# The token sums of a feed-forward block, written and streamed in interleaved orders

## The chip, the cores and the metric

The kernel runs on one core of a Trainium2 chip. The metric is the device time of one execution in microseconds (us). Two runs of the kernel before took 615.34 and 617.78 us, a median of 616.56 us.

## The reference

For 2048 tokens of 512 channels it mixes two branches with a gate per token:

```
x = A_x                                            # 2048 x 512
g = sigmoid((x * gate_w).sum(-1))
a = attention(x @ wqkv) @ wo                       # 32 heads of 16; each token sees itself and 7 tokens before, 2 apart
b = (gelu(x @ w_gate) * (x @ w_up)) @ w_down       # 512 -> 1792 -> 512
out = g * a + (1 - g) * b
```

All is float32. The change is in the operands of `x @ w_gate` and `x @ w_up`.

## The kernel before

**Tiling.** The tokens are split by parity (even and odd); each parity has 1024 tokens, in two blocks of 512. The 512 channels are four chunks of 128, and a chunk's 128 channels lie on the 128 partitions, so that a tile of x is 128 channels by 512 tokens. The 1792 hidden channels are 14 blocks of 128 (f in the code).

**Precision.** A float32 matmul is made from operands rounded to fewer bits (fp32r). Each operand is split (lines 82 to 87): ScalarE writes the rounded value `hi` (line 86), and VectorE the rest, `raw - hi` (line 87), as `lo`. A product is then three matmuls: hi by hi, hi of the weights by lo of the tokens, lo of the weights by hi of the tokens.

**Gate and up.** x times the two weight blocks of an f is taken as a 2 by 2 by 2 block product: token block by channel half, times channel half by gate or up. It is done with seven block products in place of eight (Strassen's method in Winograd's form). For this, four sums of the token blocks are needed: with a11, a12 the first token block's channel halves and a21, a22 the second's, s1 = a21 + a22, s2 = s1 - a11, s4 = a12 - s2, s3 = a11 - a21. A channel half is two chunks (kc = 0, 1), so there are eight tiles of sums. `sums_x` (lines 125 to 138) computes them on VectorE, in place, and splits each into the tile pair `XOP[name, kc]`: one tile of 1024 columns with the tag S, hi in the first 512 and lo in the last. It does so once for each token parity: before the value projection of the even tokens, and beside the key and query projection of the odd ones.

`gate_up` (lines 537 to 588) makes the seven products of one f. Four of them stream a sum (s1, s2, s4, s3), three stream a token block's half as it is (a11, a12, a22). Each call of `product` (lines 475 to 481) is six matmuls into one PSUM bank: for each of two chunks, the three of the split. The weights are the stationary operand, 128 by 128; the tokens are the moving operand, 128 by 512, one column for each token:

```python
            for n, (w_, a_) in enumerate(((wh, ah), (wh, al), (wl, ah))):
                LAST[:] = [nc.tensor.matmul(ps, w_, a_, start=(start and kc == 0 and n == 0),
```

So a sum's tiles are written once for each parity, and read by 42 matmuls (14 blocks of f times 3).

**Around it.** `ffn` runs the 14 blocks of a parity. Between the products of block f it places the down projection of earlier blocks (`down`, line 520), ScalarE's and VectorE's work on the results (lines 485 to 497, 555, 570, 586), and the preparation of the next weights (`fetch`, `combine`, `operands`, `down_w`). The attention's work on VectorE (lines 288 to 339) is a generator from which `pull` takes a bit at a time, by a written cost for each step. `paced` adds an order after the last matmul recorded, which is no wait on a value. The order of the instructions on each engine comes from this program order, as the tile framework's scheduler sets it.

Of the kernel before, what the change touches and what calls it, by code (L numbers as in the profile page):

```python
# [44 lines left out]
def tile_gated_mix(ctx: ExitStack, tc: tile.TileContext, xt, wqkv, wff, wo, out):  # L45
    nc = tc.nc
# [10 lines left out]
    def tl(tag, dt=F32):  # L57
        return pool.tile([P, COLS.get(tag, 512)], dt, name=tag, bufs=BUFS[tag])

    def pair(tag):  # L60
        t = tl(tag, F32R)
        return t[:, :512], t[:, 512:1024]
# [19 lines left out]
    def split(eng, hi, lo, raw, copy=None):  # L82
        if copy:
            copy(hi, raw)
        else:
            nc.scalar.activation(hi, raw, AF.Copy)
        eng.tensor_tensor(lo, raw, hi.bitcast(F32), op=OP.subtract)
# [13 lines left out]
    X, XOP, XR, WC = {}, {}, {}, {}  # L101
    LAST = []

    def fetch_x(par, kc):

        raw = XR[kc] = tl("raw")
        for blk in range(2):
            nc.sync.dma_start(raw[:, blk * 1024:blk * 1024 + 1024].rearrange("p (a c) -> p a c", a=2),
                                xt[2 * par + blk, :, kc:kc + 3:2, :])
# [14 lines left out]

    def sums_x():

        for n in ("s1", "s2", "s4", "s3"):
            for kc in range(2):
                XOP[n, kc] = pair("S")
        for kc in range(2):  # L130
            a11, a12, a21, a22 = (XR[kc][:, i * 512:(i + 1) * 512] for i in range(4))
            nc.vector.tensor_tensor(a22, a21, a22, op=OP.add)
            nc.vector.tensor_tensor(a21, a11, a21, op=OP.subtract)
            nc.vector.tensor_tensor(a11, a22, a11, op=OP.subtract)
            nc.vector.tensor_tensor(a12, a12, a11, op=OP.subtract)
            for n, x in ("s1", a22), ("s2", a11), ("s4", a12), ("s3", a21):
                split(nc.vector, *XOP[n, kc], x)
                yield

    def rooms():  # L140
# [333 lines left out]

    def product(ps, a, w, start):
        for kc in range(2):
            ah, al = XOP[a, kc]
            wh, wl = (x[:, kc * P:(kc + 1) * P] for x in w)
            for n, (w_, a_) in enumerate(((wh, ah), (wh, al), (wl, ah))):
                LAST[:] = [nc.tensor.matmul(ps, w_, a_, start=(start and kc == 0 and n == 0),  # L480
                                            stop=(kc == 1 and n == 2), skip_group_check=True)]

    def copy(ps):
        s = tl("s")
        nc.scalar.activation(s, ps, AF.Copy)  # L485
        return s
# [50 lines left out]
    def gate_up(par, f, pieces, do):  # L537
# [13 lines left out]
        idle(0, 0.0)  # L551
        X_ = bank("p")
        product(X_, "a11", w["b11"], True)
        W_ = bank("p")
        nc.scalar.activation(W_, X_, AF.Copy)
        idle(1, 0.7)
        piece(0)
        Z_ = bank("p")
        product(Z_, "s1", w["t1"], True)
        p5 = copy(Z_)  # L560
        idle(2, 0.3)
        fourth()
        product(X_, "s2", w["t2"], False)
        u2 = copy(X_)
        idle(3, 0.7)
# [57 lines left out]
    def ffn(par):  # L623
# [3 lines left out]
        for f in range(FC):  # L627
# [24 lines left out]
            if par:  # L652
                if f + 2 < FC:
                    at(0, fetch_sums, f + 2)
                else:
                    at(0, fetch_o) if f + 2 == FC else None
                if f + 1 == FC:
                    todo = chain(load_o(), channels_of(0, 0))
                    for i in range(1, 9):
                        at(i, next, todo, None)  # L660
            else:
                if f + 2 < FC:
                    at(1, fetch, f + 2)
                    at(8, combine, f + 2)
                else:
                    at(0, fetch_x, 1, f + 2 - FC)
                if f + 1 < FC:
                    do.setdefault(0, []).insert(0, lambda: keep(f + 1))
                at(0, keep_parts, f)
                if f + 2 == FC:  # L670
                    at(8, early)
                if f + 1 == FC:
                    todo = before()
                    for i in range(2, 9):
                        at(i, next, todo, None)
# [119 lines left out]
    for kc in range(KC):  # L795
# [4 lines left out]
        for blk in range(2):  # L800
            for a, n in first if not blk else ((0, 512),):
                o = (2 * blk + kc // 2) * 512 + a
# [16 lines left out]
    for _ in sums_x():  # L819
        pass  # L820
# [19 lines left out]
    for kc in range(KC):  # L840
        load_cb(1, kc, "c", room)()
    project(1, 0, sums_x())
    for kc in range(KC):
        load_cb(2, kc, "r", room, True)()
# [48 lines left out]
```

## Time and profile before

| | |
|---|---|
| runs | 615.34 and 617.78 us, median 616.56 |
| span of the profiled execution | 614.2 us |
| TensorE (PE) busy | 604.1 us, 98% |
| TensorE weight loads (PEld) busy | 505.3 us, 82% |
| VectorE (DVE) busy | 513.7 us, 84% |
| ScalarE (ACT) busy | 376.9 us, 61% |
| GpSimd (POOL) busy | 82.5 us, 13% |
| matmuls of line 480 that stream a sum | 672, mean 389 ns each |
| matmuls of line 480 that stream a token block | 504, mean 390 ns each |

The profile is of one execution. Its span goes from the first to the last instruction, 614.2 us; its own time isn't listed apart from the two runs, and the fastest of them is 1.1 us above the span. Matmuls are pipelined: one of 389 ns begins before the one before it has ended, so the pace is read from the distance of their starts and not from their durations. PEld, the load of the stationary operand, overlaps PE. In a row of a group stand line, engine, operation, what is written and read, shapes, count; then busy time, the mean of one, and the idle time of the engine just before them with what ended it.

### The profile page before, as it was taken

What the parts mean: (1) busy time and instruction counts of PE and PEld (TensorE: products, weight loads), DVE (VectorE), ACT (ScalarE), POOL (GpSimd) and SP (SyncE); (2) the same over time, 40 slices, a digit from 0 to 9 for tenths busy, and PEclk for the clock granted to TensorE, in tenths of its full rate; (3) what the DMA queues carried; (4) which work ended last, traced back from release to release, by engine and by line L of the source; (5) the groups of instructions that cost most, each with busy time, mean ns of one, the idle gap of its engine ahead of it and who ended that gap; (6) DMA issues with size and microseconds to landing.
All of it is one profiled execution on the core that took longest, in us unless ns stands there. A gap on an engine that the chain in (4) does not pass through costs nothing.

```text
span 614.2 us, 8246 instructions
## 1 busy us (share of the span) xinstructions
PE 604.1 (98%) x2839; PEld 505.3 (82%) x2839; DVE 513.7 (84%) x598; ACT 376.9 (61%) x633; POOL 82.5 (13%) x110
## 2 busy tenths in 40 slices
PE   9999998999999999999999999999999999999997
PEld 7899886877878888888889888888888888888885
DVE  6849699878998888756698998899899889797972
ACT  6554545674867877857356439447756676685632
POOL 0061011120212121101100002101011101101300
PEclk9999999999999999999999999999999999999999
DMA  8398949797889988995639969787888769937724
GB/s 286 98 252 253 319 145 299 192 262 226 204 225 277 305 210 219 280 231 179 237 93 330 305 174 266 210 235 186 238 200 221 162 225 215 268 86 206 91 64 154
DMA packets 85591, 132.48 MB, mean 216 GB/s; under 512 B 8111, under 2 KB 52271, under 8 KB 85550
## 3 DMA queue, kind: packets, MB, share of 16 engines
q1 hardware_dynamic: 63742, 94.27, 46.9%
q0 software_dynamic: 12672, 32.84, 28.1%
q10 hardware_dynamic: 9136, 4.85, 2.6%
q8 instruction: 22, 0.36, 0.3%
q14 instruction: 19, 0.16, 0.1%
HBM read 67.18 MB, written 36.77 MB: 169 GB/s over the span
## 4 chain that ended last, share of the span: by engine, by line
PE 81%; issue 8%; DMA 7%; DVE 3%; ACT 0%; POOL 0%; SPq 0%; POOLq 0%; DVEq 0%; ACTq 0%
PE p L480 35%; PE acc L191 15%; PE acc L520 11%; PE p L520 11%; PE p L742 5%; PE p L191 4%; DMA raw<-wff 3%; PE acc L742 2%; DMA g<-raw 2%; DMA d<-r 1%; DVE prod L326 1%; DMA raw<-xt 1%; DMA ws<-raw 1%; DVE raw L423 0%; DVE prod L330 0%
## 5 line engine op out<-in xcount | busy, mean ns | idle before, releaser
L480 PE MATMUL p<-S,g 128*128 128x512 f32 x672 | 166.6, 389 | 0.8 <-DVE c L490 0.8
L480 PEld LDWEIGHTS p<-S,g 128*128 128x128 f32 x672 | 126.0, 188 | 27.3 <-DVE c L490 1.3
L480 PE MATMUL p<-A,g 128*128 128x512 f32 x504 | 127.4, 390 | 2.9 <-ACT g L446 1.2
L480 PEld LDWEIGHTS p<-A,g 128*128 128x128 f32 x504 | 94.2, 188 | 23.9 <-DMA g<-raw 1.8
L288 DVE TENSOR_TENSOR prod<-kq 128x2048 f32<-128x2048 f32 x32 | 73.1, 2284 | 13.2 <-DMA kq<-kq 5.9
L326 DVE TENSOR_TENSOR prod<-v,lg 128x2048 f32<-128x2048 f32 x32 | 73.0, 2281 | 6.4 <-DMA v<-vs 4.9
L442 POOL DMA_DIRECT2D g<-raw x42 | 36.4, 867 | 298.3 <-ACT g L441 145.5
L291 DVE TENSOR_REDUCE lg<-prod 128x128 f32<-128x2048 f32 x32 | 73.0, 2282 | 0.3
L520 PE MATMUL p<-d,hh 128*128 128x512 f32 x224 | 68.6, 389 | 0.0
L520 PE MATMUL acc<-d,hh 128*128 128x512 f32 x224 | 60.7, 390 | 1.1 <-DMA d<-r 1.1
L520 PEld LDWEIGHTS acc<-d,hh 128*128 128x128 f32 x224 | 42.0, 188 | 10.4 <-DMA d<-r 1.4
L446 ACT ACTIVATE g<-raw 128x1024 fp32r<-128x1024 f32 (+1 forms) x42 | 41.3, 988 | 13.1 <-PE p L480 12.8
L520 PEld LDWEIGHTS p<-d,hh 128*128 128x128 f32 x224 | 42.0, 188 | 8.8
L490 DVE TENSOR_TENSOR c<-p,s 128x512 f32<-128x512 f32 x56 | 38.2, 685 | 12.9 <-PE p L480 12.6
L441 ACT ACTIVATE g<-raw 128x1024 fp32r<-128x1024 f32 (+1 forms) x42 | 41.3, 983 | 9.9 <-DVE raw L423 9.5
L485 ACT ACTIVATE s<-p 128x512 f32<-128x512 f32 x56 | 33.1, 593 | 21.4 <-PE p L480 21.2
L497 DVE TENSOR_TENSOR hl<-c,hh 128x512 fp32r<-128x512 f32 x56 | 38.0, 679 | 9.3 <-ACT hh L496 9.3
L494 DVE TENSOR_TENSOR c<-c 128x512 f32<-128x512 f32 x56 | 38.3, 685 | 8.4 <-ACT c L586 7.9
L520 PE MATMUL p<-d,hl 128*128 128x512 f32 x112 | 42.9, 389 | 0.0
L496 ACT ACTIVATE hh<-c 128x512 fp32r<-128x512 f32 x56 | 35.1, 626 | 9.7 <-DVE c L494 9.2
L533 ACT ACTIVATE rt<-p 128x512 f32<-128x512 f32 x48 | 27.9, 594 | 20.2 <-PE p L520 20.1
L191 PE MATMUL acc<-g,A 128*128 128x258 f32 (+2 forms) x228 | 39.5, 306 | 0.0
(146 smaller groups left out, 912.1 us busy)
## 6 DMA issues: line engine op xcount, KB each, us to landing
g<-raw POOLq DMA_DIRECT2D x28, 512.0 KB, 7.3
raw<-wff SPq DMA_DIRECT2D x42, 256.0 KB, 3.8
ws<-g SPq DMA_DIRECT2D x14, 768.0 KB, 5.5
g<-ws SPq DMA_DIRECT2D x14, 768.0 KB, 6.6
r<-wff SPq DMA_DIRECT2D x28, 256.0 KB, 4.3
d<-r POOLq DMA_DIRECT2D x28, 256.0 KB, 6.4
g<-raw POOLq DMA_DIRECT2D x14, 384.0 KB, 5.9
v<-vs SPq DMA_DIRECT2D x8, 512.0 KB, 7.7
```

The costliest lines, as they stand in the source:

```text
L191: LAST[:] = [nc.tensor.matmul(ps[:, :cn], a[:, t], w[:, c0:c0 + cn], start=(kc == 0 and n == 0), stop=(kc == KC - 1 and n == 2))]
L288: paced(nc.vector.tensor_tensor(prod, spans(k, jj), q[:, jj:jj + 2, None, :].to_broadcast([P, 2, W, UC]), op=OP.mult))
L291: nc.vector.tensor_reduce(two_of(lg, jj), prod.rearrange("p j w (h d) -> p (j w) h d", d=DH), axis=AX.X, op=OP.add)
L326: paced(nc.vector.tensor_tensor(prod.rearrange("p j w (h d) -> p (j w) h d", d=DH), spans(v, jj).rearrange("p j w (h d) -> p j w h d", d=D ...
L441: nc.scalar.activation(lo, raw, AF.Copy, scale=-1.0)
L446: ins = nc.scalar.activation(hi, raw, AF.Copy)
L480: LAST[:] = [nc.tensor.matmul(ps, w_, a_, start=(start and kc == 0 and n == 0), stop=(kc == 1 and n == 2), skip_group_check=True)]
L490: nc.vector.tensor_tensor(c, ps, s, op=OP.add)
L494: nc.vector.tensor_tensor(ge, ge, up, op=OP.mult)
L497: nc.vector.tensor_tensor(hl_, ge, hh_.bitcast(F32), op=OP.subtract)
L520: LAST[:] = [nc.tensor.matmul(pp, a[:, ts], w, start=(i == 0 and n == 0 and gr == 0), stop=(i == 1 and n == 2), skip_group_check=True)]
L742: LAST[:] = [nc.tensor.matmul(pa, a, b, start=(first and n == 0), stop=(last and n == 2), skip_group_check=True)]
```

## The change

A table gives an order (h, b) for 15 of the 16 sums (four names, two chunks, two parities); the s3 of the odd tokens' first chunk has none. When `sums_x` splits a sum, hi and lo are written to other columns than before, and `product` reads them with an access pattern that yields the tokens in their old order. Results and PSUM layouts stay as they were.

With b above 1 a tile of 512 columns is h regions of 512 / h columns; tokens are dealt out to the regions in runs of b. Order (2, 4), for instance, puts tokens 0 to 3 into the first half, 4 to 7 into the second, 8 to 11 into the first, and so on; whoever reads the tokens in order takes four neighbouring words, hops 256 columns (1024 bytes) on, takes four, and hops back. With b = 1 the tokens are written h columns apart, and read with a step of h words: every second or every fourth word, in two or four passes over the tile.

```diff
+    ORDER = {(0, "s1", 0): (2, 2), (0, "s1", 1): (2, 4), (0, "s2", 0): (2, 8), (0, "s2", 1): (2, 16),
+             (0, "s4", 0): (2, 32), (0, "s4", 1): (4, 2), (0, "s3", 0): (4, 4), (0, "s3", 1): (4, 16),
+             (1, "s1", 0): (2, 64), (1, "s1", 1): (8, 2), (1, "s2", 0): (8, 4), (1, "s2", 1): (4, 8),
+             (1, "s4", 0): (2, 1), (1, "s4", 1): (4, 1), (1, "s3", 1): (16, 2)}
+    SEEN = {}
+
+    def seen(t, n, kc):
+
+        o = SEEN.get((n, kc))
+        if o is None:
+            return t
+        h, b = o
+        if b == 1:
+            return t.rearrange("p (a h) -> p h a", h=h)
+        return t.rearrange("p (h a b) -> p a h b", h=h, b=b)
+
+    def shaped(t, n, kc):
+        o = SEEN.get((n, kc))
+        if o is None:
+            return t
+        h, b = o
+        if b == 1:
+            return t.rearrange("p (h a) -> p h a", h=h)
+        return t.rearrange("p (a h b) -> p a h b", h=h, b=b)
+
...
     def sums_x():
 
+        par = 1 if SEEN else 0
+        SEEN.clear()
+        SEEN.update({(n, kc): o for (q, n, kc), o in ORDER.items() if q == par})
         for n in ("s1", "s2", "s4", "s3"):
...
             for n, x in ("s1", a22), ("s2", a11), ("s4", a12), ("s3", a21):
-                split(nc.vector, *XOP[n, kc], x)
+                split(nc.vector, *(seen(y, n, kc) for y in XOP[n, kc]), shaped(x, n, kc))
                 yield
...
     def product(ps, a, w, start):
         for kc in range(2):
-            ah, al = XOP[a, kc]
+            ah, al = (seen(y, a, kc) for y in XOP[a, kc])
             wh, wl = (x[:, kc * P:(kc + 1) * P] for x in w)
```

A name of ORDER is (token parity, sum, chunk). The a11, a12 and a22 operands have no order, and are read as before.

## The prediction

> **What bounds the kernel now.** I read the page's first part, the slices and the chain of the work that ended last, in that order.
>
> ```profile
> PE 604.1 (98%) x2839; PEld 505.3 (82%) x2839; DVE 513.7 (84%) x598; ACT 376.9 (61%) x633; POOL 82.5 (13%) x110
> ...
> PE   9999998999999999999999999999999999999997
> ...
> PEclk9999999999999999999999999999999999999999
> ...
> PE 81%; issue 8%; DMA 7%; DVE 3%; ACT 0%; POOL 0%; SPq 0%; POOLq 0%; DVEq 0%; ACTq 0%
> PE p L480 35%; PE acc L191 15%; PE acc L520 11%; PE p L520 11%; PE p L742 5%; PE p L191 4%; DMA raw<-wff 3%; PE acc L742 2%; DMA g<-raw 2%; DMA d<-r 1%; DVE prod L326 1%; DMA raw<-xt 1%; DMA ws<-raw 1%; DVE raw L423 0%; DVE prod L330 0%
> ```
>
> TensorE is busy for 604.1 of 614.2 us, in every slice, at the full granted clock throughout, and the chain is TensorE for 81%. The largest part of the chain is line 480, the gate and up products. The change is about that line's streamed operand. So the first question is how much room the stage has, and I asked for the busy time by stage (columns: the stage, its length, then PE, PEld, DVE, ACT and POOL busy with their instructions, clock, DMA share, GB/s) and for what TensorE waits for.
>
> ```profile
> 18.00:60.00 42.00, 42.00 (x277) 38.73 (x276) 31.22 (x42) 21.35 (x53) 11.90 (x20) 1.00 0.72 202
> 60.00:120.00 60.00, 57.70 (x253) 47.07 (x252) 51.21 (x57) 33.00 (x51) 6.03 (x7) 1.00 0.86 249
> 120.00:180.00 60.00, 57.42 (x249) 46.21 (x249) 54.71 (x66) 40.06 (x65) 10.33 (x12) 1.00 0.87 226
> 180.00:240.00 60.00, 60.00 (x267) 49.69 (x266) 51.08 (x65) 47.22 (x74) 11.02 (x13) 1.00 0.88 240
> ...
> 300.00:330.00 30.00, 30.00 (x191) 27.18 (x190) 28.58 (x37) 19.91 (x43) 2.96 (x5) 1.00 0.65 199
> 330.00:400.00 70.00, 70.00 (x343) 59.38 (x342) 64.29 (x67) 35.95 (x62) 6.90 (x8) 1.00 0.87 248
> 400.00:460.00 60.00, 60.00 (x267) 49.67 (x266) 57.15 (x59) 38.10 (x61) 6.06 (x7) 1.00 0.82 215
> ```
>
> In the feed-forward stages TensorE has 2.30 us of gaps between 60 and 120 us, 2.58 between 120 and 180, and none after. Whatever a matmul of line 480 takes longer is therefore added to the time nearly one to one; whatever it takes shorter is gained only until VectorE (57.15 of 60 us in the later stages) becomes the bound.
>
> **The change, part by part.** Instruction for instruction, the built program has the same work in the same order on all five engines; no transfer is added or moved and no wait. What differs is the form of 15 of the 16 pairs of split instructions that write the sums (line 86 on ScalarE, line 87 on VectorE) and the order in which line 480 streams those sums. With h and b as the change's table gives them, a sum lies in h regions, and its reader takes b neighbouring words from each region in turn; for b = 1 it reads every h-th word. I sort the fifteen by the length of their runs: lone words 8 bytes apart, (2, 1), and 16 bytes apart, (4, 1); runs of two, four sums; of four, three; of eight, two; of 16 and more, four. One sum of the odd tokens (s3, first channel chunk) stays as it was.
>
> *The matmuls.* Their number and present price:
>
> ```profile
> L480 PE MATMUL p<-S,g 128*128 128x512 f32 x672 | 166.6, 389 | 0.8 <-DVE c L490 0.8
> L480 PEld LDWEIGHTS p<-S,g 128*128 128x128 f32 x672 | 126.0, 188 | 27.3 <-DVE c L490 1.3
> L191 PE MATMUL acc<-g,A 128*128 128x258 f32 x96 | 14.7, 284 | 0.0
> ```
> ```profile
> 191.35 2.72 PE p L480 x12
> ```
>
> 672 matmuls stream a sum: 16 sums (four names, two chunks, two parities) times 14 blocks times 3, so 42 for each sum, and 630 get a new order. Twelve take 2.72 us, 0.227 us from one to the next. From 258 to 512 columns an instruction grows from 284 to 389 ns, so a column streams in 105 / 254 = 0.413 ns, and the other 15 ns of the 227 are fixed.
>
> No moving operand in the trace before has a hop in it, so the price of a hop is bounded from both sides. Below: nothing, if the operand port takes any order, or even a gain of the 15 fixed ns, for which I see no reason. Above: the pace at which the other readers of the same memory take words.
>
> ```profile
> L446 ACT ACTIVATE g<-raw 128x1024 fp32r<-128x1024 f32 x28 | 29.7, 1060 | 11.8 <-PE p L480 11.5
> ...
> L446 ACT ACTIVATE g<-raw 128x768 fp32r<-128x768 f32 x14 | 11.8, 843 | 1.3 <-PE p L480 1.3
> ```
> ```profile
> L330 DVE TENSOR_TENSOR prod<-prod 128x1024 f32<-128x1024 f32 x32 | 39.0, 1219 | 0.4
> ...
> L332 DVE TENSOR_TENSOR prod<-prod 128x512 f32<-128x512 f32 x32 | 22.0, 688 | 0.5
> ```
>
> ScalarE takes a word in (1060 − 843) / 256 = 0.85 ns, VectorE in (1219 − 688) / 512 = 1.04 ns. TensorE's weight load is the slowest reader here: 128 columns in 188 ns, 1.47 ns a column, all of its fixed part counted. So line 480 is the one consumer that moves words of four bytes more than twice as fast as any other, and if that pace comes from neighbouring words being fetched together, it is the first to lose it when runs get short. I take that: runs of two and lone words 8 bytes apart fall to ScalarE's 0.85 ns, the nearest row above 0.413; lone words 16 bytes apart, which share nothing, fall to the weight load's 1.47; runs of four words and longer cost nothing.
>
> A matmul at 0.85 ns takes 512 × 0.435 = 0.223 us more, one at 1.47 ns 512 × 1.056 = 0.541 us more. Five sums (four with runs of two, and (2, 1)) are 210 matmuls: +46.8 us. The (4, 1) sum is 42 matmuls: +22.7 us. Together +69.5 us. Of the even tokens' share (two sums, 84 matmuls, 18.7 us) I take 3 us as covered by the 4.9 us of gaps shown above: what TensorE waits for there arrives at its old time while TensorE is later. The odd tokens' stages have no gap to fill. The sum is **+66.5 us**.
>
> VectorE and ScalarE are no limit then: their work in the longer stages is the same, so their shares fall, and what was late behind them (c of line 490, 0.8 us before the sums' matmuls) is late no more. The next wait is again the matmul before.
>
> *The splits.* Fifteen on each of the two engines now write with hops.
>
> ```profile
> L87 DVE TENSOR_TENSOR S<-raw,S 128x512 fp32r<-128x512 f32 x22 | 14.3, 680 | 0.0
> ...
> L87 DVE TENSOR_TENSOR hl<-raw,hh 128x512 fp32r<-128x512 f32 x8 | 5.3, 684 | 6.5 <-ACT hh L86 6.5
> ```
> ```profile
> L86 ACT ACTIVATE S<-raw 128x512 fp32r<-128x512 f32 x22 | 13.3, 629 | 10.9 <-DVE raw L134 7.3 <-DMA raw<-os 1.8 <-DVE raw L135 1.6
> ...
> L86 ACT ACTIVATE hh<-raw 128x512 fp32r<-128x512 f32 x8 | 4.8, 628 | 10.7 <-DMA raw<-os 9.1 <-PE acc L742 1.5
> ```
>
> The hh and hl rows are splits too, from line 723, and they already write in another order than they read, in runs of 32 words: 684 against 680 ns and 628 against 629 ns, so hops between long runs are free there. Short runs aren't shown; between nothing and a doubling they cost 15 × (0.629 + 0.680) = 19.6 us on two engines at most. On the path this is nothing:
>
> ```profile
> L480 PE MATMUL p<-S,g x672: 388/389/500, 59.3 to 555.6; 128*128 128x512 f32 x168
> ```
> ```profile
> 30.22 0.69 DVE L87 TENSOR_TENSOR S<-raw,S 128x512 fp32r<-128x512 f32 x1
> ```
> ```profile
> 321.66 0.67 DVE L87 TENSOR_TENSOR S<-raw,S 128x512 fp32r<-128x512 f32 x1
> ```
> ```profile
> 343.64 1.52 PE L480 MATMUL p<-S,g 128*128 128x512 f32 x6
> ```
>
> The last even sum is done at 30.9 us and first streamed at 59.3; the last odd one at 322.3 and 343.6. Doubling even all eight even and seven odd pairs, one engine after the other, takes 10.5 and 9.2 us, inside 28 and 21 us, while TensorE is busy without a gap with line 191 (42.00 of 42.00 and 30.00 of 30.00 us above). Were that cover gone, at most the 5 us that one engine loses in one parity would show.
>
> **The sum.** The profiled execution spans 614.2 us; the two runs have a median of 616.56, 2.4 us more for what lies around the span. 616.56 + 66.5 gives **683 us**. The forecast's own range is 670 (the 16-byte sum at ScalarE's pace too: 252 × 0.223 − 3 = +53) to 703 (210 matmuls at VectorE's 1.04 ns, +0.320 us each, and the same 22.7: +87).
>
> **The rivals.** *Only lone words pay.* The port needs two neighbouring words, and gets them from runs of two. Then the two sums with b = 1 remain: +9.4 us for one of them at 0.85 ns up to +9.4 + 22.7 for both, 626 to 648 us. For it: two of the 0.413 ns columns make 0.83 ns, ScalarE's time for one word, so a port at ScalarE's rate that takes two words at a time would do. Against it: nothing in the trace shows such a port.
> [...]
>
> *Every hop pays.* The operand is fetched in pieces longer than four words. If runs of eight are slow as well, five more sums, 210 matmuls, cost 46.8 us: 730 us; if all fifteen are, another 168 matmuls: 767 us. For it: 0.413 ns a column is the fastest stream of the kernel, with nothing beside it to compare with. Against it: the rows of lines 86 and 87 with hops between runs of 32 words pay nothing.
>
> *The port takes any order* (the other side: not slower). The operand's addresses are made word by word at 0.413 ns, and memory follows. Place: line 480; price nothing, 614 to 622 us. It decides as soon as the 630 matmuls lose under 12.3 us together, 20 ns each. For it: no stage of this kernel shows the operand port at a limit, since the stationary loads of 188 ns fit under the 227.
>
> [...]
>
> That the change doesn't do what it says is no rival: the writes have their new shapes in the built program.
>
> **How the numbers follow.** Forecast 0.40 (670 to 703), only lone words 0.18, every hop 0.22, any order 0.17, gain 0.03. A measurement of this kernel tells about 2%, 12.3 us, from no change. Within it lie any order, the gain for the most part (0.01 beyond), and the bottom of the lone-word case (0.05): 0.23. Slower by more: 0.40 + 0.13 + 0.22 and a little of any order, 0.76; faster 0.01. The range goes from 614, which leaves out the gain, to 735, which leaves out half of every hop: 0.14 outside. Both signs of the unknown price are in it.
>
> **What would show it.** In the profile after, the product line's matmuls of the sums would have a mean between 389 and some 500 ns, and in the order of time the groups of sums with runs of two or lone words would start 0.45 us apart, (4, 1) some 0.77, all other sums and the a11, a12, a22 products 0.227 as before. TensorE's busy share stays at 98%, VectorE's falls to about 76%. The forecast is wrong if runs of two keep 0.227 us, or runs of four and more lose it; a longer time with matmuls at the old spacing would mean that the splits weren't covered.

## The result and the profile after

The changed kernel takes 673.27 us (673.06 to 673.49, two runs) against 616.56 us: the ratio is 1.091, with a 95% interval from 1.0843 to 1.0976. That is 56.7 us more. The forecast was 683 us, its own range 670 to 703.

The page of the changed kernel, its first part, slices and chain:

```profile
PE 665.9 (99%) x2839; PEld 509.4 (76%) x2839; DVE 517.3 (77%) x598; ACT 380.3 (57%) x633; POOL 82.5 (12%) x110
...
PE   9999999999999999999999999999999999999997
...
PE 96%; DMA 2%; ACT 1%; DVE 0%; issue 0%; SPq 0%; ACTq 0%
PE p L509 49%; PE acc L220 15%; PE acc L549 11%; PE p L549 11%; PE p L771 5%; PE p L220 3%; PE acc L771 2%; DMA c<-wqkv 1%; DMA raw<-xt 1%; ACT s L557 1%; DVE hl L526 0%; DVE S L87 0%; ACT S L191 0%; ACT hl L242 0%; ACT p L543 0%
```

The chain is now TensorE for 96%, and the product line (509, which was 480) alone is 49% of the span. TensorE's gaps shrank from 614.2 − 604.1 = 10.1 us to 671.3 − 665.9 = 5.4. The groups of that line:

```profile
L509 PE MATMUL p<-S,g 128*128 128x512 f32 x672 | 229.0, 488 | 0.0
...
L509 PE MATMUL p<-A,g 128*128 128x512 f32 x504 | 127.6, 391 | 0.0
```

The matmuls that stream a sum went from a mean of 389 to 488 ns; those that stream a plain block stayed (390 and 391). What one order costs can be read from the weight loads in order of time: there is one for each matmul, and here their rows stand apart. These six belong to one product of the odd tokens (s4), whose two chunks have the orders (2, 1) and (4, 1); the columns are start, length, instruction, count, and the idle time before:

```profile
480.78 0.19 PEld L509 LDWEIGHTS p<-S,g 128*128 128x128 f32 x1
481.22 0.21 PEld L509 LDWEIGHTS p<-S,g 128*128 128x128 f32 x1 [0.25 <-issue]
481.67 0.21 PEld L509 LDWEIGHTS p<-S,g 128*128 128x128 f32 x1 [0.24 <-issue]
482.12 0.21 PEld L509 LDWEIGHTS p<-S,g 128*128 128x128 f32 x1 [0.24 <-issue]
482.58 0.21 PEld L509 LDWEIGHTS p<-S,g 128*128 128x128 f32 x1 [0.25 <-issue]
483.04 0.21 PEld L509 LDWEIGHTS p<-S,g 128*128 128x128 f32 x1 [0.25 <-issue]
```

The first three are 0.44 and 0.45 us apart and the next three 0.46: lone words 8 bytes apart and 16 bytes apart cost nearly the same. Taken over the whole trace, from each matmul's start to the next (mean of 42, and 42 times what is above 0.227 us):

| order | ns to the next | us in all |
|---|---|---|
| (2, 2) | 334 | 4.5 |
| (4, 2), (16, 2) | 446, 450 | 9.2, 9.4 |
| (8, 2) | 512 | 12.0 |
| (2, 1) | 446 | 9.2 |
| (4, 1) | 460 | 9.8 |
| (2, 4), (4, 4), (8, 4) | 255, 268, 280 | 1.2, 1.7, 2.2 |
| (2, 8), (4, 8) | 244, 233 | 0.7, 0.2 |
| (2, 16), (4, 16), (2, 32), (2, 64) | 240, 235, 236, 227 | 0.6, 0.3, 0.4, 0.0 |

The six short orders make 54.1 us, the nine others 7.3. Less the 4.7 us of gaps that were filled, this is 56.7 us. The one sum left in its plain order stands at 235 ns here, right behind (4, 1). So the rows of 235 and 236 ns need not be the price of their own hops: some of it may be left over from the matmuls before.

### The profile page after: what moved, and what is told of

The parts are those of the page before. It is cut to its first block, busy times and chain, and to the rows that moved or that the text cites. A ratio compares the mean times of both kernels' runs of the same rounds, so it can differ in the third digit from the quotient of the medians.

```text
span 671.3 us, 8246 instructions
## 1 busy us (share of the span) xinstructions
PE 665.9 (99%) x2839; PEld 509.4 (76%) x2839; DVE 517.3 (77%) x598; ACT 380.3 (57%) x633; POOL 82.5 (12%) x110
## 4 chain that ended last, share of the span: by engine, by line
PE 96%; DMA 2%; ACT 1%; DVE 0%; issue 0%; SPq 0%; ACTq 0%
PE p L509 49%; PE acc L220 15%; PE acc L549 11%; PE p L549 11%; PE p L771 5%; PE p L220 3%; PE acc L771 2%; DMA c<-wqkv 1%; DMA raw<-xt 1%; ACT s L557 1%; DVE hl L526 0%; DVE S L87 0%; ACT S L191 0%; ACT hl L242 0%; ACT p L543 0%
## 5 line engine op out<-in xcount | busy, mean ns | idle before, releaser
L509 PE MATMUL p<-S,g 128*128 128x512 f32 x672 | 229.0, 488 | 0.0
L509 PEld LDWEIGHTS p<-S,g 128*128 128x128 f32 x672 | 130.0, 194 | 69.3 <-issue 37.4
L500 POOL DMA_DIRECT2D d<-r x28 | 24.1, 883 | 128.8 <-ACT d L499 104.5
L359 DVE TENSOR_TENSOR prod<-prod 128x1024 f32<-128x1024 f32 x32 | 39.0, 1220 | 0.4
```

The source lines that it names most:

```text
L359: nc.vector.tensor_tensor(prod[:, :, :4], prod[:, :, :4], prod[:, :, 4:], op=OP.add)
```

## Experiments: where the time is lost

**Writing alone.** The products read each tile plainly; the tiles are still written in the new orders.

```diff
-            ah, al = (seen(y, a, kc) for y in XOP[a, kc])
+            ah, al = XOP[a, kc]
```

> The sums are written in their new orders, but the products stream each tile from its first to its last column. What is left out: the tokens of a sum are not put back into their order, so the gate and up products of different tokens are added. Theory (the whole cost is in the streaming of line 480): 614 to 620 us, matmuls that stream a sum at a mean of 389 ns as before, the split rows of the sums a little longer than 680 and 629 ns. Rival (the fifteen split pairs with hops hold something up): above 625 us with matmuls at 389 ns.

Measured: 614.42 us, ratio to the kernel before 0.999 (0.997 to 1.0011). VectorE's rows of the sums, in this run:

```profile
L87 DVE TENSOR_TENSOR S<-raw,S 128x512 fp32r<-128x512 f32 x22 | 14.8, 705 | 0.0
```

```profile
L509 PE MATMUL p<-S,g 128*128 128x512 f32 x672 | 166.6, 389 | 0.8 <-DVE c L519 0.8
```

The splits in this group (22, of which 16 are the sums') grew from a mean of 680 to 705 ns, and none of it shows in the time: the whole loss is in the streaming.

**The long orders alone, and the short ones alone.** The table keeps only these entries; nothing else is changed:

```diff
+    ORDER = {(0, "s1", 1): (2, 4), (0, "s2", 0): (2, 8), (0, "s2", 1): (2, 16),
+             (0, "s4", 0): (2, 32), (0, "s3", 0): (4, 4), (0, "s3", 1): (4, 16),
+             (1, "s1", 0): (2, 64), (1, "s2", 0): (8, 4), (1, "s2", 1): (4, 8)}
```

> The six sums with runs of two words or lone words keep their plain order; the nine with runs of four and longer keep the new one. Theory (runs of four and more cost nothing, short ones all of it): 615 to 620 us. Rival (every hop costs a little, whatever the run): the 27 to 53 ns that the matmuls with runs of four take longer in the changed kernel, 126 of them, and some 8 to 17 ns for the other 252, make 5 us and 3 us, so 621 to 625 us.

Measured: 622.02 us beside 615.39 for the kernel before, ratio 1.0099 (1.0063 to 1.0134), 6.6 us. The rival holds (621 to 625 us): long orders aren't free, but cheap.

```diff
+    ORDER = {(0, "s1", 0): (2, 2), (0, "s4", 1): (4, 2),
+             (1, "s1", 1): (8, 2), (1, "s4", 0): (2, 1), (1, "s4", 1): (4, 1), (1, "s3", 1): (16, 2)}
```

> The six sums with runs of two or lone words have their new orders, the nine others the plain one. By the rows of the changed kernel the six lose 4.5, 9.2, 12.0, 9.2, 9.8 and 9.4 us, 54 us together, less the 4.9 us of gaps that the streaming now fills: 662 to 668 us. Rival (the long orders' 6.6 us are not lost beside the short ones, since they too fill gaps): 670 to 674 us.

Measured: 666.38 us beside 614.47, ratio 1.0827 (1.0783 to 1.0871), 51.9 us. That is within the 662 to 668 us expected. The two parts, 6.6 and 51.9, add up to the change's 56.7 within 2 us.

## Experiments: what makes an order dear

Run length does not explain the table: (2, 2) and (8, 2) have the same runs and lose 107 and 285 ns. So whole tables of orders were tried, 42 matmuls for each, with tiles named by their order so that each has a row. Each table ran once; the rows of its trace are read, not its time.

**Lone words and runs of two, by the number of regions and the hop.** The reader's access pattern got a number of free words behind each region. To make room for them the tile S is 1088 columns wide in place of 1024, and the width of another kind of tile (WA) went from 576 to 516. This moves tiles to other places in memory, and matmuls that no order touches are slower by it or by something else in the edit: the 48 of the query, key and value projection with the operands S and A (p<-S,A) take 394 ns here and in the two other tables made so, against 389 before. So differences of some 5 ns between these tables and the plain 389 aren't those of an order.

```diff
-        return t.rearrange("p (h a b) -> p a h b", h=h, b=b)
+        return bass.AP(a.tensor, a.offset, [a.ap[0], [b, 512 // (h * b)], [512 // h + pad, h], [1, b]])
```

> Another table of orders, with a third number, the words left free behind each region, and tiles named by their order: lone words with steps of 2, 8, 16, 64, 128 and 256 words; runs of two with 2, 4, 8, 32, 64 and 128 regions, some with 4, 8 or 16 free words, which shift the hop by one, two or four steps of 16 bytes; one plain sum. Theory 'length': a word that is not in a run of four goes alone, at 0.85 ns, wherever the hop leads: every row but the plain one has a mean near 621 to 640 ns. Rival 'place': runs of two are fetched together, and what costs is a hop onto the same part of the memory: rows of runs of two lie between 389 and 700 ns by their hop, those with 4 free words near 389, and lone words of a large step differ from those of a small one.

The groups of the product line (a tile h4b2p4o0s has 4 regions, runs of 2, 4 free words, no shift):

```profile
L518 PE MATMUL p<-h64b1p0o0s,g 128*128 128x512 f32 x42 | 24.5, 710 | 0.0
...
L518 PE MATMUL p<-h128b2p0o0s,g 128*128 128x512 f32 x42 | 21.4, 628 | 0.0
L518 PE MATMUL p<-h2b1p0o0s,g 128*128 128x512 f32 x42 | 21.4, 629 | 0.0
L518 PE MATMUL p<-h4b2p4o0s,g 128*128 128x512 f32 x42 | 21.3, 629 | 0.0
...
L518 PE MATMUL p<-h8b1p0o0s,g 128*128 128x512 f32 x42 | 20.7, 612 | 0.0
...
L518 PE MATMUL p<-h2b2p4o0s,g 128*128 128x512 f32 x42 | 16.3, 502 | 0.0
...
L518 PE MATMUL p<-h128b1p0o0s,g 128*128 128x512 f32 x42 | 14.2, 444 | 0.0
...
L518 PE MATMUL p<-h1b512p0o0s,g 128*128 128x512 f32 x42 | 12.4, 401 | 0.0
...
L518 PE MATMUL p<-h256b1p0o0s,g 128*128 128x512 f32 x42 | 11.4, 379 | 0.0
```

Both theories fall. Lone words and runs of two lie anywhere between 379 and 710 ns, where length alone would have them all near 630. Four free words move no row of runs of two to 389 ns (629, 502), so the hop's place isn't it either. And the last row has no two neighbouring words at all: 256 regions, lone words, so the reader takes words 0, 256, 1, 257, 2, and so on. It is the fastest, 379 ns, 216 ns from one matmul to the next, less than a plain tile's 227 in the kernel before (and 389 ns; 401 for the plain tile of this table).

**Runs of four and shifts.** A fourth number moves the tile by so many words (the tiles are as wide as in the table before):

```diff
+        a = t[:, off:off + 512]
```

> A third table of orders; a fourth number shifts the whole tile by so many words. Runs of four with 2, 4, 8 and 32 regions, with 4 free words, and shifted by 1 and 2 words so that a run crosses a step of 16 bytes; a plain sum shifted by 1 and by 2 words; runs of two shifted by 1; runs of 8 and 64; one plain sum. Theory 'length': a shift changes nothing: plain rows 389 ns, runs of four 400 to 450, runs of two 510 to 690. Rival 'steps of 16 bytes': a run of four that crosses a step is two pieces, so shifted runs of four rise to 600 ns or more while the unshifted stay below 450; shifted plain sums stay at 389.

```profile
L518 PE MATMUL p<-h4b4p0o2s,g 128*128 128x512 f32 x42 | 23.4, 675 | 0.0
L518 PE MATMUL p<-h4b4p0o1s,g 128*128 128x512 f32 x42 | 21.3, 641 | 0.0
...
L518 PE MATMUL p<-h4b4p0o0s,g 128*128 128x512 f32 x42 | 13.6, 434 | 0.0
...
L518 PE MATMUL p<-h1b512p0o1s,g 128*128 128x512 f32 x42 | 12.3, 398 | 0.0
...
L518 PE MATMUL p<-h1b512p0o2s,g 128*128 128x512 f32 x42 | 11.9, 392 | 0.0
```

The same runs of four cost 434 ns when they fill a step of 16 bytes, and 641 or 675 when they are shifted by one or two words and cross one; a plain tile hardly minds the shift (398 and 392, against 392 unshifted). So in these rows the 16-byte step counts, and the rival of this run holds. But why is a run of two, with two words of a step, slow (496 to 651 ns in the table before), and one word in turn from two halves the fastest (379)?

**Two streams.** The account formed from these rows is a way of counting: a matmul's even columns (0, 2, 4 ...) and odd columns (1, 3, 5 ...) are taken as two streams, and for each it is counted how many words in a row lie in the same 16 bytes. In a run of two, each stream has one (496 to 651 ns). In 0, 256, 1, 257, the even stream reads 0, 1, 2, 3 and the odd one 256, 257, 258, 259: four each (379). In unshifted runs of four it is two each (434 with four regions). A shift of these by one word leaves one of the streams one word on each side of the step (641), a shift by two words leaves both so (675). The author's guess was that a row is slow where a stream has fewer than two. The next table was made for this account alone, with tiles as wide as in the kernel before; here an order is a nest of steps and counts, and its name spells it, outermost first:

```diff
+    def ap(t, dims):
+        return bass.AP(t.tensor, t.offset, [t.ap[0], *([s, c] for s, c in dims if c > 1)])
```

> A fourth table of orders; an order is now a nest of steps and counts, outermost first, and tiles are named by it (x4n128 is a step of 4 words, 128 times). Theory 'two streams': the even and the odd columns of a matmul are fetched apart, and each is at full pace if it takes two words or more from 16 bytes before it leaves them; four are better than two. It expects means near 378 ns (as the order 0, 256, 1, 257 of the sweep before, with four each) for 0, 256, 1, 257 again, 0, 4, 1, 5, for 0, 8, 1, 9, and for alternating words 128, 64, 32 and 16 apart; near 389 for lone words two apart taken in turn from two halves (0, 256, 2, 258, two each) and for 0, 2, 1, 3; near 620 for lone words four or eight apart taken in turn from two halves (one each); 490 to 510 for the runs of two in two regions again, and more than 389 for 0, 2, 4, 6, 1, 3, 5, 7, where each stream changes its 16 bytes at every word. Rival 'open places': what counts is how many 16-byte steps are in use at once, at most two: 0, 256, 2, 258 is then like 0, 256, 1, 257 and so is the order with lone words four apart from two halves, near 389, and 0, 2, 1, 3 is at full pace too.

```profile
L514 PE MATMUL p<-s,g 128*128 128x512 f32 x84 | 23.9, 389 | 0.0
L514 PE MATMUL p<-x1n8x8n32x256n2s,g 128*128 128x512 f32 x42 | 21.8, 635 | 0.0
L514 PE MATMUL p<-x1n4x4n64x256n2s,g 128*128 128x512 f32 x42 | 21.2, 625 | 0.0
...
L514 PE MATMUL p<-x8n64x1n2x2n4s,g 128*128 128x512 f32 x42 | 16.5, 509 | 0.0
L514 PE MATMUL p<-x2n128x256n2x1n2s,g 128*128 128x512 f32 x42 | 16.5, 506 | 0.0
L514 PE MATMUL p<-x1n128x128n4s,g 128*128 128x512 f32 x42 | 14.3, 446 | 0.0
...
L514 PE MATMUL p<-x4n128x1n2x2n2s,g 128*128 128x512 f32 x42 | 12.4, 399 | 0.0
...
L514 PE MATMUL p<-x1n2x2n128x256n2s,g 128*128 128x512 f32 x42 | 11.8, 389 | 0.0
L514 PE MATMUL p<-x8n64x1n4x4n2s,g 128*128 128x512 f32 x42 | 11.6, 381 | 0.0
L514 PE MATMUL p<-x32n16x1n16x16n2s,g 128*128 128x512 f32 x42 | 11.5, 379 | 0.0
L514 PE MATMUL p<-x1n256x256n2s,g 128*128 128x512 f32 x42 | 11.5, 379 | 0.0
```

| columns read | words of the even stream | in one 16 bytes | expected, measured ns |
|---|---|---|---|
| 0, 256, 1, 257 | 0, 1, 2, 3 | 4 | 378, 379 |
| 0, 4, 1, 5, 2, 6 | 0, 1, 2, 3 | 4 | 378, 381 |
| 0, 256, 2, 258 | 0, 2, 4, 6 | 2 | 389, 389 |
| 0, 2, 1, 3 | 0, 1, then 4, 5 | 2 | 389, 399 |
| 0, 256, 4, 260 | 0, 4, 8 | 1 | 620, 625 |
| 0, 256, 8, 264 | 0, 8, 16 | 1 | 620, 635 |

By runs and hops the rows that alternate between two halves can't be told apart, and they lie from 379 to 635 ns as the count says. The rival "open places" fell with the 625 ns: two places are in use there as in the rows of 379 and 389. Nor does it do to count the words in the same 16 bytes over neighbouring columns: lone words 8 bytes apart and runs of two in 128 regions have two in a row, and took 629 and 628 ns in the table of lone words and runs of two.

Three half-way rows are not covered by the plain account: runs of two in two regions (506 ns), 0, 2, 4, 6, 1, 3, 5, 7 (x8n64x1n2x2n4, 509 ns) and 0, 128, 256, 384, 1 (x1n128x128n4, 446 ns). In each of them a stream alternates between two places and uses each again, and loses about half (506, 509) or a quarter (446) of the 236 to 246 ns that the rows of 625 and 635 lose against 389. Why wasn't tried apart. The account also says only which orders are dear, and not how dear: where each stream takes one word and goes on, the two tables that try it have rows from 611 to 651 ns, lone words 64 apart, whose streams go round four places and come back, have 710, and (8, 2) costs more than (4, 2) and (16, 2) in the changed kernel. The two streams are read out of the rows alone: no view of the trace shows how the words are fetched.

**Hops of runs of four and more.** What is left of the price there, 7.3 us of the change:

> A fifth table: runs of four and longer by the place that the hop leads to, with free words behind the regions. Two streams alone leave nothing for these rows: each stream finds two words in each 16 bytes, so all are at 389 to 395 ns. Rival (place): hops of 1024, 512 and 256 bytes are dear, 409, 432 and 445 ns for runs of four as in the sweep before, and the rows with free words, whose hops are no multiple of 256 bytes, are at 389 to 400 ns.

```profile
L518 PE MATMUL p<-h8b4p0o0s,g 128*128 128x512 f32 x42 | 14.1, 442 | 0.0
...
L518 PE MATMUL p<-h4b8p4o0s,g 128*128 128x512 f32 x42 | 12.8, 415 | 0.0
...
L518 PE MATMUL p<-h2b4p8o0s,g 128*128 128x512 f32 x42 | 12.5, 405 | 0.0
...
L518 PE MATMUL p<-h8b4p4o0s,g 128*128 128x512 f32 x42 | 12.2, 395 | 0.0
L518 PE MATMUL p<-h4b4p4o0s,g 128*128 128x512 f32 x42 | 12.2, 395 | 0.0
L518 PE MATMUL p<-h4b8p0o0s,g 128*128 128x512 f32 x42 | 12.2, 394 | 0.0
```

Inconclusive. Four free words take (8, 4) from 442 to 395 ns and (4, 4) from 434 in the sweep before to 395, as the rival says, but they take (4, 8) from 394 to 415, and no free words bring (2, 4) below 405. The place of a hop seems to matter by some 10 to 50 ns, and by what rule stays open. What stands around a row matters too: (8, 8) had 425 ns in the table with the shifts and 406 in this one, with the same sum and other neighbours. Nor do two words in a row from 16 bytes keep a stream at the plain pace in all of these rows (390 to 442 ns for the runs of four), as the plain account would have it.

## Experiments: reading from two halves on purpose

The row of 379 ns is a gain of 11 ns a matmul (216 ns from start to start in place of 227), for a kernel whose bound is the pace of matmuls. Four runs tried to collect it.

**The change with one order.** All sixteen sums get (256, 1):

```diff
+    ORDER = {(q, n, kc): (256, 1) for q in range(2) for n in ("s1", "s2", "s4", "s3") for kc in range(2)}
```

> The change with one order for all sixteen sums: 256 regions, lone words, so that a sum's reader takes words in turn from the two halves of the tile. From the sweep's row with that order: 216 ns from one matmul to the next in place of 227, 672 times: 7.4 us less than before, 607 to 610 us. Rival (a gain of single rows is lost behind them, to the gaps or to VectorE): 614 to 617 us.

Measured: 614.11 us beside 615.43, ratio 0.9984 (0.9967 to 1.0). The pace came as expected: the busy time of the sums' matmuls fell from 166.6 to 159.3 us, 10.9 ns for each of the 672. But TensorE's busy time fell by 604.1 − 599.0 = 5.1 us and not by 7.4, and its gaps rose from 10.1 to 612.3 − 599.0 = 13.3 us: the rival holds. All sixteen sums are written as lone words here. ScalarE is busy for 381.7 us and VectorE for 519.3, against 376.9 and 513.7 before; and the projections' matmuls with the operands g and A (acc<-g,A, 228 of them) wait for 1.1 us, 0.7 of it for ScalarE, where they waited for nothing before. So some of the loss may be the writing's, which wasn't tried apart; the next run writes nothing in another order.

**All seven products.** Nothing is stored in another order; every token tile is read from two halves, so PSUM and the hidden blocks hold the tokens as 0, 256, 1, 257, and the down projection picks its 128 stationary tokens with a step of two:

```diff
+    def halves(t):
+        return t.rearrange("p (h a) -> p a h", h=2)
-            ah, al = XOP[a, kc]
+            ah, al = (halves(y) for y in XOP[a, kc])
+    def of_tokens(a, t):
+        return a.rearrange("p (a h) -> p h a", h=2)[:, t // 2, t % 2 * P:(t % 2 + 1) * P]
...
-                LAST[:] = [nc.tensor.matmul(pp, a[:, ts], w, start=(i == 0 and n == 0 and gr == 0),
+                LAST[:] = [nc.tensor.matmul(pp, of_tokens(a, t), w, start=(i == 0 and n == 0 and gr == 0),
```

> No order is written at all. All seven products stream their token tiles, sums and plain blocks, by words in turn from the two halves (0, 256, 1, 257); the hidden blocks then lie in that order of tokens, and the down projection takes its stationary tokens with a step of two columns. 1176 matmuls with 11 ns less: 12.9 us less than before, 601 to 606 us, if the weight load with a step of two is no slower than 188 ns or stays under the matmul. Rival (the stepped weight load takes twice as long, and shows): the 672 matmuls of the down projection at 376 ns or more, over 680 us.

Measured: 610.19 us, ratio 0.9906 (0.9889 to 0.9922). The groups of the products and of the down projection:

```profile
L483 PE MATMUL p<-S,g 128*128 128x512 f32 x672 | 159.6, 379 | 1.3 <-DVE c L493 1.0 <-ACT s L488 0.2
L483 PE MATMUL p<-A,g 128*128 128x512 f32 x504 | 122.2, 380 | 4.3 <-ACT g L449 1.7 <-DMA g<-raw 1.4 <-DVE c L493 1.2
L525 PE MATMUL p<-d,hh 128*128 128x512 f32 x224 | 70.2, 395 | 0.0
```

All 1176 product matmuls gain. The down projection's lose, 395 for 389 ns; the busy time of their four rows grew from 208.5 to 213.2 us. Its stepped weight loads take 194 for 188 ns. That the loads are the reason isn't shown: in the next run they take 196 ns, and the same matmuls, with their moving operand read in halves, take 379 (the median). Gaps are 14.2 us. So 5 of the 13 us arrive, and the 601 to 606 us expected are missed; the rival's loads of twice the length didn't come.

**All matmuls.** The moving weights of the other products are laid out in two halves as well, which the launch does with their columns, and read by `halves`:

```diff
+    def parted(w):
+        w = np.asarray(w)
+        return w.reshape(*w.shape[:-1], -1, 2).swapaxes(-1, -2).reshape(w.shape)
-    wff = np.concatenate([cols(B_w_gate), cols(B_w_up), kchunks(B_w_down)], 2)
+    wff = np.concatenate([cols(B_w_gate), cols(B_w_up), parted(kchunks(B_w_down))], 2)
...
-                LAST[:] = [nc.tensor.matmul(ps[:, :cn], a[:, t], w[:, c0:c0 + cn], start=(kc == 0 and n == 0),
+                LAST[:] = [nc.tensor.matmul(ps[:, :cn], a[:, t], halves(w[:, c0:c0 + cn]), start=(kc == 0 and n == 0),
...
```

> As the run with all seven products, and the other matmuls' moving weights (down projection, query, key and value projection, output projection) stream by words in turn from two halves as well; their columns are laid out for it ahead of the launch, in the order of the inputs. 2520 matmuls of 512 columns with 11 ns less and 288 of 256 or 258 with half of that: 27 to 29 us less than before, 586 to 592 us. Rival (VectorE, at 57 of 60 us busy in the odd tokens' feed-forward stage, becomes the bound): 595 to 603 us.

Measured: 597.67 us (597.07 to 598.48), ratio to the kernel before 0.9709 (0.9695 to 0.9724). It beats both kernels, and misses the 586 to 592 us expected; the time lies in the rival's range. The first line of its page:

```profile
PE 576.5 (97%) x2839; PEld 507.4 (85%) x2839; DVE 512.0 (86%) x598; ACT 373.2 (63%) x633; POOL 82.7 (14%) x110
```

TensorE is busy 27.6 us less, as expected, but its gaps rose from 10.1 to 19.3 us, which leaves 18. Who it waits for, and the odd tokens' stage (VectorE is the third pair of numbers after the length):

```profile
PE p L483 <- DVE c L493: 2.9, 3, 1.1
PE p L483 <- DMA g<-raw: 2.8, 4, 1.4
PE acc L525 <- DMA d<-r: 2.5, 4, 1.1
PE p L483 <- ACT g L449: 1.7, 1, 1.7
```
```profile
390.00:450.00 60.00, 57.28 (x264) 49.83 (x263) 58.60 (x60) 39.51 (x63) 6.06 (x7) 1.00 0.82 216
```

VectorE is busy for 58.60 of 60 us there: the rival's bound is near, though transfers and ScalarE share the gaps, so that VectorE alone is the bound isn't shown. With both operands stepped, the down projection's matmuls take 379 ns (the median; 389 before), with weight loads of 196 ns.

**Attention's pace.** The budgets by which attention's steps are placed were made smaller with the matmuls:

```diff
-PACE = (0.9, 1.12)
+PACE = (0.86, 1.07)
-            pull((2.7, 2.2)[par])
+            pull((2.57, 2.1)[par])
```

> As the run with all moving operands read from two halves, and the budgets by which attention's work on VectorE is placed between the matmuls are made smaller by the same 5 in 100 as the matmuls. Theory (TensorE's gaps grew from 10.1 to 19.3 us since too much of VectorE's other work stands ahead of what TensorE waits for): 592 to 596 us. Rival (the gaps come from transfers and from VectorE's whole load): 597 to 600 us.

Measured: 603.3 us, ratio to the kernel before 0.9807 (0.9767 to 0.9847), 5.6 us slower than the run with all matmuls, and outside both ranges. The work that was put off came due at the end:

```profile
PE p L747 <- ACT hh L86: 5.6, 1, 5.6
PE p L483 <- DVE c L493: 3.1, 3, 1.5
```

The output projection now waits 5.6 us for the last attention block, and the wait for VectorE is as before. The granted clock, as a mean of each of the four executions, is 0.989 to 0.993, against 0.999 to 1.0 in the run with all matmuls; how much of the longer time that makes isn't shown. The theory that attention stood too far ahead falls.

## Why the prediction was right, step by step

The bound, the direction and the size came as forecast, 673 against 683 us. Part of the closeness is luck: one term was 12.9 us too high and another 7.3 too low, and inside the five sums two misses partly offset each other.

- **TensorE is the bound, and a longer product is paid one to one.** Right. 61.4 us of longer matmuls made 56.7 us; 4.7 us went into gaps, where the prediction had 3.
- **The five sums at ScalarE's pace, +46.8 us.** 44.3 in all: the size was right and so was the pace, since (2, 1), (4, 2) and (16, 2) lie at 446 to 450 ns where the step gave 450. Two of five were off, (2, 2) with half the price and (8, 2) with a quarter more. The reason doesn't fit: if the pace came from words which follow each other being fetched together, 0, 256, 1, 257 would be slow (it is the fastest, 379 ns), and runs of two would cost less than lone words (446 and 450 ns from start to start for (4, 2) and (16, 2), 446 for (2, 1)). No run ties the price to ScalarE's pace either; that 446 and 450 agree is luck as far as the runs show.
- **The 16-byte order, +22.7 us.** The mis-sized term: +9.8 us. The weight load's 1.47 ns a column was taken as the price of a lone word; that row counts a fixed part, as the prediction says, and belongs to another instruction. That words 16 bytes apart share nothing was the author's assumption; no row of before showed it. At 460 ns from start to start the order costs nearly what lone words 8 bytes apart cost, which is what the lower end of the forecast's range, 670 us, was worked out from. The 12.9 us too much are more than the 9.8 by which the whole sum was high; the next term took most of the rest back.
- **Runs of four and more at nothing.** Wrong by 7.3 us in the trace, 6.6 us when alone. The prediction had named this as a sign of being wrong: runs of four lost the 0.227 us and stand at 0.255 to 0.280.
- **The splits are hidden.** Right: 0.999 with the writing alone.
- **The rivals.** "Every hop pays" is true of runs of four and eight, and far smaller than priced. "Only lone words pay" fell: runs of two pay as much. A gain was given 0.03; no order of the change is one, but (256, 1) in the table of lone words is, 11 ns a matmul. Whether these are part of the 15 ns that the prediction named as fixed isn't shown.

## What to carry to other kernels

The order in which a matmul's moving operand is read is a price of its own, and a large one: from 216 to over 500 ns for the same 512 float32 (fp32r) columns. Judge an access pattern by its even and its odd columns apart: in the rows where a stream changed its 16 bytes after each word, the matmul took 444 to 710 ns here against 389 to 401 for the plain one, with two in a row 387 to 444 ns, and alternating between two halves, which needs no data moved where the order of the columns is free, was faster than reading straight through (379 ns). When a bound engine gets faster by a few per cent, look at once for what stood just behind it: here only 18 of 28 us arrived.

## What the runs showed of the hardware

Reading float32 (fp32r) columns straight through is not the fastest way: 227 ns against 216 for 512 columns, at every distance tried between the alternating words, from 8 to 256 (379 ns each) and at 4 (381).

After matmuls that read in pieces, plain ones can go on being slower for a while: mostly 227 to 236 ns from start to start for the ten matmuls behind (2, 16) in the changed kernel at 184 us, and 255, 240 and 235 for the plain sum right behind (4, 1). Why wasn't looked into.

Writing lone words 16 bytes apart is dear as well, but for the writers: the split of the (4, 1) sum took 1167 ns on ScalarE and 1112 on VectorE, against 629 and 680, while lone words 8 bytes apart, (2, 1), took 677 and 675, and the splits with runs of two stayed below 750.
